# The tail of a decode layer: softmax sums ahead of the last PV, an output projection moved under a multiply, a shorter LN mean

## The chip, the cores and the metric

One core of one Trainium2 chip runs the whole program. Times are device microseconds (us), the median of several executions. The span that a profile shows, from the first to the last instruction, is about 1.8 us shorter than the time of the same execution. A verdict compares executions of fast state alone, with a 95% interval.

## The reference, cut to what matters

Two sequences decode one token through one layer. Attention reads the last 2048 positions of K and V for 32 heads of 192; then come the output projection, the residual, a second LayerNorm and a GELU feed-forward part.

```python
W = min(4096, max(256, Sk // 4))                     # Sk = 8192, so W = 2048
q = (x @ wq).reshape(B, Sq, Hq, Dh).transpose(0, 2, 1, 3)   # B=2, Sq=1, Hq=32, Dh=192
scores = jnp.einsum("bhqd,bhkd->bhqk", q, k[:, :, Sk - W:]) * (Dh ** -0.5)
o = jnp.einsum("bhqk,bhkd->bhqd", softmax(scores), v[:, :, Sk - W:])
h = x + o.reshape(B, Sq, Hq * Dh) @ wo               # D = 640; x is layer-normed ahead of wq
h2 = h + (gelu(ln(h) @ w_gate) * (ln(h) @ w_up)) @ w_down    # F = 1536
```

All tensors are bf16. Nearly all the bytes are K, V and weights, 122 MB, and each is used once.

## The kernel before

PE is TensorE (matmuls), DVE is VectorE and ACT is ScalarE; a load has landed when all of it is in SBUF. PV is the product of the exp of the scores with V. The o rows are its results summed into rows; the orow multiply divides them by the sums of exp and spreads them over the heads; the o columns are the same values turned, so that they can be multiplied with `wo`. The h columns and h rows are the residual sum h in the two layouts that the LayerNorm and the output need.

The kernel records its operations with the tiles they read (R), write (W) and the PSUM banks they touch (X); waits between engines follow from that. All loads but the small x go through one ring in SBUF and one DMA queue; the last of them, in a fixed order, are the end of K and V (16 steps, of which four make a group J of eight heads), then `wo` of heads 16 to 23, `wo` of heads 24 to 31, gate, up, and down in four quarters. After the last V nothing streams but the rest of these weights. The tail from there on is what the change rewrites.

```python
        def pv(g):
            ...                                  # 32 matmuls into ops_
            if g % 4 == 3:
                act(lambda e: e.activation(out=osb[:, :], in_=ops_[:, 0:384], func=ACT.Copy), W=["osb"], X=["o"])

        def o_rows(J):
            def fn(e):
                for tp in range(2):
                    e.matmul(m1[:, 0:DH], lhsT=selw[:, tp, :], rhs=osb[:, DH * tp:DH * (tp + 1)], ...)
                return e.matmul(m2[:, 272:276], lhsT=zsel[:, :], rhs=zr[:, J % 2, :], start=True, stop=True)
            pe(fn, ...)                          # o rows, then the sums of exp
            ...                                  # DVE: z4, rinv, wm
            dve(tt(orow[:, :, :], m1[:, 0:DH]..., wm[:, :]..., ALU.mult), R=["wm"], W=["orow"], X=["m1"])
        ...
        o_rows(3)
        o_columns(3)                             # 12 matmuls, then a small copy to ot
        oproj(2)                                 # wo of heads 16 to 23, into bank m1
        oproj(3)                                 # wo of heads 24 to 31, then hrow = m1 + hrow
        h_columns()
        layernorm(hT, "hT", hnT[:, :, :].unsqueeze(2), "hnT")
        ...
        ffn_in(sps, "s", "wg")                   # gate
        pe(h_rows, ...)                          # h into the bank of the output
        gT = ffn_columns(sps, "s", 0)            # an ACT and a DVE copy, then 3 transposes
        ...
        ffn_in(ops_, "o", "wu")                  # up, then down in four groups
```

(Cuts are marked by dots.)

Of the kernel before, what the change touches and what calls it, by code (L numbers as in the profile page):

```python
# [6 lines left out]
F32 = mybir.dt.float32  # L7
I32 = mybir.dt.int32
ALU = mybir.AluOpType
# [3 lines left out]
B = 2  # L13
# [137 lines left out]
def bass_sequential_preLN__sliding_block_cached__geglu_ffn__decode_kernel(  # L151
# [12 lines left out]
    with ExitStack() as ctx:  # L164

        def sb(name, shape, dt):
            return ctx.enter_context(nc.sbuf_tensor(name, shape, dt))
# [39 lines left out]
        lt = sb("lt", [128, 2, B], F32)  # L207
        xnT = sb("xnT", [128, NC5, 136], BF16)
        hnT = sb("hnT", [128, NC5, B], BF16)
        hT = sb("hT", [128, NC5, B], F32)  # L210
        qrow = sb("qrow", [128, 2, 2, DH], BF16)
        rq = sb("rq", [128, NG, 6, 16], BF16)
        mx = sb("mx", [128, 1], F32)
# [143 lines left out]

        dve(lambda e: e.memset(xnT[:, :, :].rearrange("p a b -> p (a b)").bitcast(I32), 0), W=["xnT"])

        def layernorm(src, src_tok, dst, dst_tok):  # L360
            dve(lambda e: e.tensor_reduce(out=ls[:, 0, :], in_=src[:, :, :].rearrange("p c b -> p b c"), axis=AX.X,
                                          op=ALU.add), R=[src_tok], W=["ls0"])
            pe(lambda e: e.matmul(m2[:, 16:18], lhsT=onesd[:, :], rhs=ls[:, 0, :], start=True, stop=True),
               R=["onesd", "ls0"], X=["m2"])
            dve(tt(dT[:, 0, :, :], src[:, :, :], m2[:, 16:18].unsqueeze(1).to_broadcast([128, NC5, B]), ALU.subtract),
                R=[src_tok], W=["dT0"], X=["m2"])
            dve(tt(dT[:, 1, :, :], dT[:, 0, :, :], dT[:, 0, :, :], ALU.mult), R=["dT0"], W=["dT1"])
            dve(lambda e: e.tensor_reduce(out=ls[:, 1, :], in_=dT[:, 1, :, :].rearrange("p c b -> p b c"), axis=AX.X,
                                          op=ALU.add), R=["dT1"], W=["ls1"])
            pe(lambda e: e.matmul(m2[:, 20:22], lhsT=onesd[:, :], rhs=ls[:, 1, :], start=True, stop=True),  # L370
               R=["onesd", "ls1"], X=["m2"])
            act(lambda e: e.activation(out=lt[:, 0, :], in_=m2[:, 20:22], func=ACT.Ln, bias=eps_t[:, :], scale=1.0),  # L372
                R=["eps"], W=["lt0"], X=["m2"])
            act(lambda e: e.activation(out=lt[:, 1, :], in_=lt[:, 0, :], func=ACT.Exp, scale=-0.5), R=["lt0"], W=["lt1"])
            n = dst.shape[2]
            dve(tt(dst, dT[:, 0, :, :].unsqueeze(2).to_broadcast([128, NC5, n, B]),
                   lt[:, 1, :].unsqueeze(1).unsqueeze(1).to_broadcast([128, NC5, n, B]), ALU.mult), R=["dT0", "lt1"], W=[dst_tok])
# [6 lines left out]

        pe(_x_T, R=["xrow", "identb"], X=["m2"])
        dve(lambda e: e.tensor_copy(xT[:, :, :].rearrange("p c b -> p (c b)"), m2[:, 0:10]), W=["xT"], X=["m2"])
        layernorm(xT, "xT", xnT[:, :, :].rearrange("p c (j x) -> p c j x", j=4)[:, :, :, 0:B], "xnT")


        dve(tt(pti[:, :], pi[:, :].to_broadcast([128, 11]), bits[:, :], ALU.bitwise_and),  # L390
# [44 lines left out]
        def consts_late():  # L435
            dve(ts(oh4[:, :], cf[:, 0, 0:4], pg[:, 8:9], ALU.is_equal), R=["cf0", "cq"], W=["oh4"])
            dve(ts(cf[:, 1, :], cf[:, 1, :], 2.0, ALU.mult), R=["cfm", "mska"], W=["cf1"])
            dve(ts(cf[:, 4, :], cf[:, 4, :], 0.25, ALU.mult), R=["cfm"], W=["cf4"])
            dve(tt(cf[:, 1, :], cf[:, 1, :], cf[:, 4, :], ALU.add), R=["cf1", "cf4"], W=["cf1"])
            dve(ts(cf[:, 3, :], cf[:, 3, :], 1000.0, ALU.mult), R=["cfm", "pm"], W=["cf3"])  # L440
            dve(tt(cf[:, 1, :], cf[:, 1, :], cf[:, 3, :], ALU.add), R=["cf1", "cf3"], W=["cf1"])
            for tp in range(2):
                dve(ts(selw[:, tp, :], cf[:, 1, :], float(tp), ALU.add, rb(31), ALU.is_equal), R=["cf1", "pf"], W=[("selw", tp)])
            for h in range(2):
                dve(ts(hsel[:, h, :], cf[:, 0, 0:2], 32.0 * h, ALU.add, pg[:, 12:13], ALU.is_equal), R=["cf0", "c63"], W=[("hsel", h)])
            dve(ts(pg[:, 8:9], rb(32), 1.0 / 32.0, ALU.mult), R=["pf", "cqb", "oh4"], W=["cb"])
            dve(ts(selb[:, :], cf[:, 0, 0:2], pg[:, 8:9], ALU.is_equal, pg[:, 2:3], ALU.mult), R=["cf0", "cb", "v4"], W=["selb"])
            dve(ts(maskhd[:, :], cf[:, 0, 0:8], pg[:, 10:11], ALU.is_equal, pg[:, 2:3], ALU.mult),
                R=["cf0", "chd", "v4"], W=["maskhd"])
# [109 lines left out]
        def pv(g):  # L559
            vv, vtoks = where["v", g]  # L560

            def fn(e):
                for t in range(32):
                    r = t % 4
                    ins = e.matmul(ops_[32 * r:32 * (r + 1), 0:384], lhsT=ering[:, g % 4, t, :],  # L565
                                   rhs=vv[:, 384 * t:384 * (t + 1)], start=(g % 4 == 0 and t < 4),
                                   stop=(g % 4 == 3 and t >= 28),
                                   tile_position=(0, 32 * r), skip_group_check=True)
                return ins

            pe(fn, R=[("er", g % 4)] + vtoks, X=["o"])
            done(("v", g))
            if g % 4 == 3:
                act(lambda e: e.activation(out=osb[:, :], in_=ops_[:, 0:384], func=ACT.Copy), W=["osb"], X=["o"])

        def o_rows(J):
            def fn(e):
                for tp in range(2):
                    e.matmul(m1[:, 0:DH], lhsT=selw[:, tp, :], rhs=osb[:, DH * tp:DH * (tp + 1)], start=(tp == 0),  # L579
                             stop=(tp == 1), skip_group_check=True)  # L580
                return e.matmul(m2[:, 272:276], lhsT=zsel[:, :], rhs=zr[:, J % 2, :], start=True, stop=True)

            pe(fn, R=["osb", "zsel", ("selw", 0), ("selw", 1)] + [("zr", J % 2, k) for k in range(4)], X=["m1", "m2"])
            dve(lambda e: e.tensor_tensor_reduce(out=z4[:, :], in0=m2[:, 272:276], in1=oh4[:, :], scale=1.0, scalar=0.0,
                                                 op0=ALU.mult, op1=ALU.add, accum_out=zs[:, :]), R=["oh4"], W=["z4", "zs"], X=["m2"])
            dve(lambda e: e.reciprocal(rinv[:, :], zs[:, :]), R=["zs"], W=["rinv"])
            dve(ts(wm[:, :], maskhd[:, :], rinv[:, 0:1], ALU.mult), R=["maskhd", "rinv"], W=["wm"])
            dve(tt(orow[:, :, :], m1[:, 0:DH].unsqueeze(1).to_broadcast([128, 8, DH]),
                   wm[:, :].unsqueeze(2).to_broadcast([128, 8, DH]), ALU.mult), R=["wm"], W=["orow"], X=["m1"])

        def o_columns(J):
            def fn(e):
# [7 lines left out]
        def oproj(J):  # L600
# [16 lines left out]
            done(("wo", J))  # L617
            if J == 0:
                dve(lambda e: e.tensor_copy(hrow[0:98, :], m1[0:98, 192:512]), W=["hrow"], X=["m1"])
            if J % 2:  # L620
                dve(tt(hrow[0:98, :], m1[0:98, 192:512], hrow[0:98, :], ALU.add), R=["hrow"], W=["hrow"], X=["m1"])

        def h_columns():
            def fn(e):
                for c in range(NC5):
                    for h in range(2):
                        ins = e.matmul(m2[64 * h:64 * h + 64, 32 + 2 * c:34 + 2 * c], lhsT=hrow[0:98, c:320:NC5],
                                       rhs=hsel[0:98, h, :], start=True, stop=True, tile_position=(0, 64 * h))
                return ins

            pe(fn, R=["hrow", ("hsel", 0), ("hsel", 1)], X=["m2"])
            dve(lambda e: e.tensor_copy(hT[:, :, :].rearrange("p c b -> p (c b)"), m2[:, 32:42]), W=["hT"], X=["m2"])


        transposes(0, 0)
# [6 lines left out]
        for g in range(NG):  # L642
            nxt = g + 1 < NG
            J = g // 4 - 1 if g % 4 == 0 and g > 0 else None
            if nxt:
                transposes(g + 1, 0)
            e_columns(g)
            if J is not None:
                o_columns(J)
            if nxt:  # L650
# [8 lines left out]
            if nxt:  # L659
                softmax(g + 1)  # L660
        o_rows(3)
        o_columns(3)
        oproj(2)
        oproj(3)

        h_columns()
        layernorm(hT, "hT", hnT[:, :, :].unsqueeze(2), "hnT")

        def ffn_in(bank, xt, key):
            wv, wtoks = where[key]  # L670
# [8 lines left out]
            pe(fn, R=["hnT"] + wtoks, X=[xt])  # L679

        def ffn_columns(bank, xt, i):
            act(lambda e: e.activation(out=grow[0:98, 192:384], in_=bank[0:98, 192:384], func=ACT.Copy), W=[("grow", 1)], X=[xt])
            dve(lambda e: e.tensor_copy(grow[0:98, 0:192], bank[0:98, 0:192]), W=[("grow", 0)], X=[xt])

            def fn(e):
                for j in range(3):
                    ins = e.transpose(tps[i][:, 128 * j:128 * j + 98], grow[0:98, j:384:3], identf[0:98, 0:98])  # L687
                return ins

            pe(fn, R=[("grow", 0), ("grow", 1), "identf"], X=[("t", i)])  # L690
            return tps[i][:, 0:384].rearrange("p (j r y) -> p r j y", j=3, y=32)[:, :, :, 0:2]

        def h_rows(e):
# [6 lines left out]
            return t.rearrange("p (r j b) -> p r j b", r=4, j=3)  # L700

        ffn_in(sps, "s", "wg")
        pe(h_rows, R=["hrow", ("hsel", 0), ("hsel", 1)], X=["m1"])
        gT = ffn_columns(sps, "s", 0)
        dve(lambda e: e.tensor_copy(rjb(gsb[:, :]), gT), W=["gsb"], X=[("t", 0)])
        dve(tt(ga[:, 0, :], gsb[:, :], gsb[:, :], ALU.mult), R=["gsb"], W=["ga0"])
        dve(ts(ga[:, 1, :], ga[:, 0, :], 0.044715, ALU.mult, 1.0, ALU.add), R=["ga0"], W=["ga1"])
# [83 lines left out]
```

## Time and profile before

The time is 297.32 us (three executions, 297.21 to 297.4). One execution was profiled; it took 298.14, its span is 296.4. This is 0.8 above the median.

The page of the kernel before, first line and the rows of its 40 slices: granted clock of PE and DMA share in tenths, and GB/s.

```profile
span 296.4 us, 4893 instructions
...
PEclk9996559996979589989788699979795979795555
DMA  7999999999999999999999999999999999999980
GB/s 272 435 446 433 425 425 427 428 427 435 437 413 442 428 426 417 435 437 429 427 429 433 423 425 437 431 427 425 431 430 428 423 438 430 428 424 427 423 359 37
...
```

DMA is busy throughout, at about 427 GB/s, and stops near 290 us. The last four slices have the clock of PE at half (5).

The chain of waits of the kernel before, from 255 us on (start, duration, what).

```profile
...
235.05 32.67 DMA ring<-in_A_v_cache_dram
...
267.85 2.77 PE ops L565 x32
...
271.19 1.65 PE m L579 x4
...
273.77 1.77 DVE orow L324
...
275.59 0.86 PE m L594 x12
276.45 3.33 PE m L611 x48
...
280.35 1.32 PE m L627 x20
...
284.80 1.80 PE sps L675 x15
...
288.22 1.73 PE ops L675 x20
...
291.93 1.80 PE m L722 x48
...
```

Up to 267.7 us the chain is a load. From there on it goes from engine to engine: PV, o rows, the orow multiply, o columns, both `wo` parts in one row of 48 matmuls, h columns, gate, up, down. No load stands in this part of the chain. The landings, taken from the trace's transfer records, say how near they are:

| weights | landed | first use in this profile | to spare |
|---|---|---|---|
| wo of heads 16 to 23 | 272.30 | 276.38 | 4.1 |
| wo of heads 24 to 31 | 276.89 | 277.93 | 1.05 |
| gate | 281.51 | 284.80 | 3.3 |
| up | 286.11 | 288.15 | 2.0 |
| down, last quarter | 290.79 | after 291.93 | over 1.1 |

### The profile page before, as it was taken

Reading aid. Unit: us, or ns where it says so; the run is one execution under the profiler, and the core shown is the slowest. Engines: PE = TensorE matmul, PEld = TensorE weight load, DVE = VectorE, ACT = ScalarE, POOL = GpSimd, SP = SyncE. Lnnn points to the kernel's source line nnn. Section 1 sums busy time; section 2 is a strip of 40 time slices with the busy share of each in tenths; the row PEclk is TensorE's granted clock in tenths of the full one; section 3 lists DMA queues with packets and bytes.
Section 4 is the critical chain, followed back from the end, with each engine's and each line's share of the span. In section 5 each row is a group of like instructions: output and inputs, shape, how many; then the busy total and the mean of one; then the engine's idle time right before and its main releaser. Section 6 shows DMA issues by size and latency. Waiting matters only on the chain.

```text
span 296.4 us, 4893 instructions
## 1 busy us (share of the span) xinstructions
PE 199.5 (67%) x2141; PEld 155.9 (53%) x2141; DVE 127.9 (43%) x316; ACT 98.4 (33%) x125; POOL 2.7 (1%) x19
## 2 busy tenths in 40 slices
PE   2573668849595398749492787576777885856764
PEld 1451266719393386547481766274757683834432
DVE  5950456614355154435344355334463543441222
ACT  2150134714353053416171325334334353330010
POOL 3000000000000000000000000000000000000000
PEclk9996559996979589989788699979795979795555
DMA  7999999999999999999999999999999999999980
GB/s 272 435 446 433 425 425 427 428 427 435 437 413 442 428 426 417 435 437 429 427 429 433 423 425 437 431 427 425 431 430 428 423 438 430 428 424 427 423 359 37
DMA packets 6521, 122.61 MB, mean 414 GB/s; under 512 B 738, under 2 KB 740, under 8 KB 1252
## 3 DMA queue, kind: packets, MB, share of 16 engines
q1 hardware_dynamic: 6488, 122.29, 96.8%
q8 instruction: 17, 0.28, 0.4%
q14 instruction: 4, 0.03, 0.0%
q10 hardware_dynamic: 12, 0.00, 0.0%
HBM read 122.29 MB, written 0.00 MB: 413 GB/s over the span
## 4 chain that ended last, share of the span: by engine, by line
DMA 69%; PE 24%; DVE 4%; ACT 1%; issue 1%; SPq 1%; DVEq 0%; ACTq 0%
DMA ring<-in_A_k_cache_dram 37%; DMA ring<-in_A_v_cache_dram 22%; PE tps L467 14%; DMA ring<-in_A_wq_dram 9%; PE ops L565 3%; PE m L611 1%; DVE rq L324 1%; PE m L594 1%; SPq L269 1%; PE m L722 1%; PE sps L675 1%; DVE orow L324 1%; PE ops L675 1%; PE m L579 1%; PE tps L687 1%
## 5 line engine op out<-in xcount | busy, mean ns | idle before, releaser
L467 PE MATMUL tps<-identf,ring 128*128 128x128 f32 x768 | 117.4, 323 | 47.4 <-DMA ring<-in_A_k_cache_dram 46.8
L467 PEld LDWEIGHTS tps<-identf,ring 128*128 128x128 f32 x768 | 108.2, 169 | 50.5 <-DMA ring<-in_A_k_cache_dram 48.1
L476 ACT ACTIVATE ktr<-tps 128x1024 bf16<-128x1024 bf16 x80 | 79.5, 1023 | 85.1 <-PE tps L467 85.1
L479 DVE COPY ktr<-tps 128x1024 bf16<-128x1024 bf16 x112 | 74.1, 688 | 74.3 <-PE tps L467 73.3
L540 ACT ACTIVATE eexp<-sm,nm 128x512 bf16<-128x512 f32 x16 | 11.5, 721 | 65.2 <-DVE nm L538 65.2
L565 PE MATMUL ops<-ring,ering 128*32 128x384 bf16 x512 | 25.0, 339 | 6.1 <-DMA ring<-in_A_v_cache_dram 6.0
L529 DVE CUSTOM_DVE_ANT_1 sm<-sps,mska 128x512 f32<-128x512 f32 x16 | 11.1, 691 | 40.2 <-PE sps L523 40.2
L523 PE MATMUL sps<-ktr,rq 128*16 128x512 bf16 x384 | 25.8, 403 | 0.3 <-DVE rq L324 0.3
L565 PEld LDWEIGHTS ops<-ring,ering 128*32 128x32 bf16 x512 | 12.9, 99 | 15.0 <-DMA ring<-in_A_v_cache_dram 6.4
L523 PEld LDWEIGHTS sps<-ktr,rq 128*16 128x16 bf16 x384 | 9.5, 90 | 11.3 <-issue 2.0
L536 PEld LDWEIGHTS m<-mrhs,pm 128*128 128x128 bf16 x16 | 1.5, 96 | 24.2 <-DVE mrhs L320 23.2
L536 PE MATMUL m<-mrhs,pm 128*128 128x16 bf16 x16 | 2.9, 184 | 16.8 <-DVE mrhs L320 16.0
L489 PE MATMUL tps<-ring,xnT 128*32 128x384 bf16 x80 | 5.7, 444 | 7.6 <-DMA ring<-in_A_wq_dram 7.6
L324 DVE TENSOR_TENSOR rq<-ops,mask 128x96 bf16<-128x96 f32 x16 | 2.7, 246 | 14.6 <-PE ops L507 14.6
L324 DVE TENSOR_TENSOR ering<-m,mask 128x256 bf16<-128x256 f32 x16 | 6.7, 420 | 3.5 <-PE m L549 3.5
L489 PEld LDWEIGHTS tps<-ring,xnT 128*32 128x32 bf16 x80 | 2.4, 120 | 10.4 <-DMA ring<-in_A_wq_dram 8.3
L324 DVE TENSOR_TENSOR orow<-m,wm 128x1536 bf16<-128x1536 f32 x4 | 7.0, 1757 | 0.1
L594 PE MATMUL m<-selb,orow 128*128 128x2 bf16 x48 | 3.4, 199 | 4.1 <-DVE orow L324 2.5
L372 ACT ACTIVATE lt<-m,eps_t 128x2 f32<-128x2 f32 x2 | 0.5, 262 | 16.8 <-PE m L370 16.8
L549 PE MATMUL m<-sel,eexp 128*128 128x64 bf16 x64 | 5.1, 207 | 1.2 <-ACT eexp L540 1.2
L549 PEld LDWEIGHTS m<-sel,eexp 128*128 128x128 bf16 x64 | 4.8, 112 | 1.7 <-DVE nm L538 1.3
L594 PEld LDWEIGHTS m<-selb,orow 128*128 128x128 bf16 x48 | 3.1, 159 | 4.6 <-DVE orow L324 2.6
(107 smaller groups left out, 81.3 us busy)
## 6 DMA issues: line engine op xcount, KB each, us to landing
ring<-in_A_k_cache_dram SPq DMA_DIRECT2D x16, 3072.0 KB, 26.6
ring<-in_A_v_cache_dram SPq DMA_DIRECT2D x16, 3072.0 KB, 30.1
ring<-in_A_wo_dram SPq DMA_DIRECT2D x4, 1920.0 KB, 30.9
ring<-in_A_wq_dram SPq DMA_DIRECT2D x2, 3072.0 KB, 21.1
ring<-in_B_w_gate_dram SPq DMA_DIRECT2D x1, 1920.0 KB, 33.7
ring<-in_B_w_up_dram SPq DMA_DIRECT2D x1, 1920.0 KB, 25.6
ring<-in_B_w_down_dram SPq DMA_DIRECT2D x4, 480.0 KB, 27.5
ring<-in_A_wq_dram SPq DMA_DIRECT2D x1, 1536.0 KB, 27.9
```

What stands on the lines that cost most here:

```text
L324: return lambda e: e.tensor_tensor(out=out, in0=a, in1=b, op=op)
L467: ins = e.transpose(tps[bi][:, 128 * u:128 * (u + 1)], kv[:, off:off + 128], identf[:, :])
L476: act(lambda e, dst=dst, bv=bv: e.activation(out=dst, in_=bv, func=ACT.Copy), W=[("kt", slot, n)], X=[("t", bi)])
L479: dve(lambda e, dst=dst, bv=bv: e.tensor_copy(dst, bv), W=[("kt", slot, n)], X=[("t", bi)])
L489: ins = e.matmul(tps[0][32 * r:32 * (r + 1), 0:384], lhsT=xnT[:, c, 32 * J:32 * (J + 1)], rhs=wq[:, c - c0, 1536 * J + 384 * r:1536 * J + ...
L523: ins = e.matmul(sps[32 * ch:32 * ch + 16, :], lhsT=rq[:, g, k, :], rhs=ktr[:, g % 2, k // 2, 1024 * ch + k % 2:1024 * (ch + 1):2], start= ...
L529: dve(lambda e: e.tensor_tensor_reduce(out=sm[:, :].rearrange("p (u x) -> p u x", u=4), in0=sps[:, :].rearrange("p (u x) -> p u x", u=4), ...
L540: act(lambda e: e.activation(out=eexp[:, :], in_=sm[:, :], func=ACT.Exp, bias=nm[:, 0:1], scale=1.0, accum_out=zr[:, g // 4 % 2, g % 4:g % ...
L549: ins = e.matmul(o, lhsT=eexp[:, 128 * u:128 * (u + 1)], rhs=sel64[:, :], start=True, stop=True)
L565: ins = e.matmul(ops_[32 * r:32 * (r + 1), 0:384], lhsT=ering[:, g % 4, t, :], rhs=vv[:, 384 * t:384 * (t + 1)], start=(g % 4 == 0 and t < 4),
L594: ins = e.matmul(m2[:, 2 * kk:2 * kk + 2], lhsT=orow[:, :, kk:DH:12], rhs=selb[:, :], start=True, stop=True)
L675: ins = e.matmul(bank[32 * r:32 * r + 2, 0:384], lhsT=hnT[:, c, :], rhs=wv[:, c, 384 * r:384 * (r + 1)], start=(c == 0), stop=(c == NC5 - ...
```

## The change

It has three parts. **Front:** the sums of exp, their inverse and the head mask `wm` are made before the last PV; `osb` is copied by DVE in two halves, so that the first o-row matmul can start behind the first half; the last o rows go to the bank of the scores, which leaves bank m1 free, so that `wo` of heads 16 to 23 is multiplied while DVE spreads the o rows. **Mean:** the hrow addition also sums its rows; one matmul makes the LN mean from these sums, right behind the h columns, and the copy hT goes. **FFN:** one DVE copy in place of an ACT and a DVE copy, and the h rows stand behind the gate's transposes.

```diff
-                act(lambda e: e.activation(out=osb[:, :], in_=ops_[:, 0:384], func=ACT.Copy), W=["osb"], X=["o"])
+                for tp in range(2):
+                    dve(lambda e, tp=tp: e.tensor_copy(osb[:, DH * tp:DH * (tp + 1)], ops_[:, DH * tp:DH * (tp + 1)]), ...)
...
+        def z_rows(J):                           # matmul of the sums, z4, rinv, wm: taken out of o_rows
...
+            bank, tok = (m1, "m1") if J < 3 else (sps, "s")
...
+            if J == 3:
+                dve(lambda e: e.tensor_tensor_reduce(out=hrow[0:98, :], in0=m1[0:98, 192:512], in1=hrow[0:98, :], ...,
+                                                     op0=ALU.add, op1=ALU.add, accum_out=rs[0:98, :]), ...)
...
-            dve(lambda e: e.tensor_copy(hT..., m2[:, 32:42]), W=["hT"], X=["m2"])
...
             e_columns(g)
+            if g % 4 == 3:
+                z_rows(g // 4)
...
         o_rows(3)
+        oproj(2)
         o_columns(3)
-        oproj(2)
         oproj(3)
 
         h_columns()
-        layernorm(hT, "hT", hnT[:, :, :].unsqueeze(2), "hnT")
+        layernorm(m2[:, 32:42]..., [], ["m2"], hnT[:, :, :].unsqueeze(2), "hnT",
+                  lambda e: e.matmul(m2[:, 16:18], lhsT=rs[0:98, :].to_broadcast([98, 128]), rhs=bsel[0:98, :], ...))
...
-            act(lambda e: e.activation(out=grow[0:98, 192:384], in_=bank[0:98, 192:384], func=ACT.Copy), ...)
-            dve(lambda e: e.tensor_copy(grow[0:98, 0:192], bank[0:98, 0:192]), ...)
+            dve(lambda e: e.tensor_copy(grow[0:98, :], bank[0:98, 0:384]), W=["grow"], X=[xt])
...
         ffn_in(sps, "s", "wg")
+        gT = ffn_columns(sps, "s", 0)
         pe(h_rows, R=["hrow", ("hsel", 0), ("hsel", 1)], X=["m1"])
-        gT = ffn_columns(sps, "s", 0)
```

Why the two copies of an eviction stood in sequence before, and why the last o rows need another bank for `wo` to run meanwhile: the program makes an operation wait for the last one of any other engine on the same bank (X), reads included. The trace of before agrees: ACT's half of the gate's copy runs from 286.62 to 286.95, DVE's starts at 287.05.

## The prediction

> **What bounds the kernel.** The page shows DMA 90% busy or more in nearly every slice up to slice 38, at about 427 GB/s[...], so nothing can be won while K and V stream. The chain of waits runs through DMA to 267.7 us, when the last V lands. Then comes a serial tail of 28.7 us: PV, o rows, o columns, wo, LN, FFN. The change shortens this tail alone. But weights still stream under it. By the transfer records they land at: wo of heads 16–23 272.3, wo of 24–31 276.9, gate 281.5, up 286.1, down 287.3/288.5/289.6/290.8. These times don't depend on the change. Before, the uses begin at 276.4, about 278.1, 284.8, 288.2 and 291.9.

> **The sum** (timeline and chain; the clock granted in the tail is 0.5):
> 1. Sums of exp ahead of PV: the z matmul (0.23) and z, inverse, wm (about 0.9) leave the chain. The osb copy goes from one ACT copy (0.50) to two DVE copies of about 0.36 (as the 98x192 copy took), the second behind the first o-row matmul: about even. The orow multiply starts near 272.75 instead of 273.77: −1.0.
> 2. wo of 16–23 (1.67 of the 3.33) runs under the orow multiply (1.76), in another bank. So o columns end near 275.4 and wo of 24–31 could start near 275.7, 2.4 earlier than before. But its weights land at 276.9: it starts near 277.0 and ends near 278.7 instead of 279.75. Of about 2.1 us, steps 1 and 2 together keep 1.1.
> 3. The hrow add becomes an add with a row sum (a 512-wide one took 0.69 plus its accumulator read; for 320 I estimate 0.58 against 0.49): +0.1.
> 4. Mean: hT copy, reduce and their hand-overs go. The mean matmul follows on the h columns (as the z matmul did, about 0.25), then a small mean copy (0.17): −0.6. The gate matmuls start near 283.2, not 284.8.
> 5. FFN evictions: ACT 0.34 then DVE 0.37 in sequence (same bank) become one DVE copy of 384; from 192 (0.36) and 320 (0.49) columns I estimate 0.56: −0.25 for gate, −0.25 for up.
> 6. h rows now stand behind the gate's transposes, so 0.53 of them falls between those and the up matmuls, where before they filled the eviction wait: +0.5.

> Up starts near 286.9 (landed 286.1), down near 290.4; its last quarter is needed near 291.7 (landed 290.8). No further weight binds. Elsewhere (three earlier o rows, x's LN, one more constant) the work lies under DMA: 0.

> −1.1 +0.1 −0.6 −0.25 +0.5 −0.25 = −1.6; I say 1.5.

> **Predicted:** 295.8 us, range 295.1 to 296.7. Faster by over 2% (below 291.4) 0.01, within 2% 0.98, slower 0.01. Even with all compute of the tail free, the last down weights at 290.8 plus output leave at most some 2.5 us.

> **Right if:** the first o-row matmul starts near 271.1 and orow near 272.75; wo of 24–31 waits for DMA, with PE idle over 1 us after the o columns; gate starts at 283.2±0.3; the h rows lie between transposes and up; landings are unchanged within 0.3; final copy ends near 292.5.

> **Wrong if:** the added DVE work in the K stages delays a load's issue (landings shift); wo of 24–31 doesn't wait; the row-sum add or the mean matmul costs much more than estimated; or up or down starts waiting for its weights.

(The cut took out a ceiling for DMA that no trace of this case shows. That nothing can be won while K and V stream then rests on the busy share alone and is the author's estimate. No term of the sum is cut: it came to −1.6, and 1.5 was said.)

## The result, and the profile after

| | median us | executions | lowest to highest |
|---|---|---|---|
| before | 297.36 | 6 | 297.21 to 297.73 |
| changed | 297.02 | 6 | 296.43 to 297.19 |

The ratio is 0.9983, with an interval of 0.997 to 0.9996. (A ratio is the mean time of one kernel's fast runs over that of the other's in the same rounds, so not quite the ratio of the medians; "slower" executions below are still fast runs, 0.3% apart from the rest.) The change is a gain, of 0.34 us by the medians and 0.5 by the ratio (interval 0.1 to 0.9), where 1.5 was predicted; 297.02 lies above the predicted range, which ends at 296.7.

The page of the changed kernel, first line and the rows of its slices.

```profile
span 295.2 us, 4895 instructions
...
PEclk9995959997979689977998697979599979599555
DMA  7999999999999999999999999999999999999991
...
```

The chain of waits of the changed kernel, from 230 us on (start, duration, what).

```profile
...
247.30 29.64 DMA ring<-in_A_wo_dram
...
277.07 1.80 PE m L622 x23
...
279.45 1.30 PE m L641 x20
280.75 0.53 PE m L683 x2
...
283.56 1.80 PE sps L691 x20
...
285.38 0.57 DVE grow L698
...
286.75 0.65 PE m L710 x8
287.40 1.62 PE ops L691 x20
...
290.76 1.80 PE m L737 x45
...
```

In these two profiles the gain is 296.36 − 295.25 = 1.1 us, and most events behind the o rows are close to those predicted: gate starts at 283.56 (predicted 283.2±0.3), `wo` of heads 24 to 31 now stands in the chain as a load (landed 276.94, matmuls from 277.07), the h rows stand between transposes and up. No landing moved by more than 0.06 us against before. So the profiles tell of 1.1 us and the timed medians of 0.34. The question is where the rest went.

The profile after has a second oddity. Here is its tail's front in the timeline (start, duration, engine, line, operation, what it makes from what; in brackets how long the engine was idle before it, and for whom).

```profile
...
267.97 1.48 PE L572 MATMUL ops<-ring,ering 128*32 128x384 bf16 x32
...
269.50 0.62 DVE L582 COPY osb<-ops 128x192 f32<-128x192 f32 x2 [0.79 <-PE ops L572]
...
269.91 0.92 PE L597 MATMUL sps<-osb,selw 128*128 128x192 f32 x4 [0.46 <-DVE osb L582]
270.94 1.76 DVE L326 TENSOR_TENSOR orow<-sps,wm 128x1536 bf16<-128x1536 f32 x1 [0.82 <-PE sps L597]
...
272.38 1.57 PE L622 MATMUL m<-ring,ot 128*2 128x320 bf16 x24 [1.55 <-DMA ring<-in_A_wo_dram]
...
277.07 1.77 PE L622 MATMUL m<-ring,ot 128*2 128x320 bf16 x24 [2.31 <-DMA ring<-in_A_wo_dram]
...
```

PV took 1.48 us and the o rows 0.92, where the profile of before has 2.75 and 1.65. The same 32 and 4 matmuls do the same work in both kernels. The clock was full here (1.00 from 258.98 to 272.63), half there (0.50 from 266.94 to the end), and so the first o-row matmul came at 269.91 where 271.1 was predicted. And despite that advantage of 2 us, PE then waited 1.55 us for the first `wo` part and 2.31 us for the second.

### The profile page after: what moved, and what is told of

It is laid out like the page before. It is cut to its first block, busy times and chain, and to the rows that moved or that the text cites. A ratio compares the mean times of both kernels' runs of the same rounds, so it can differ in the third digit from the quotient of the medians.

```text
span 295.2 us, 4895 instructions
## 1 busy us (share of the span) xinstructions
PE 194.2 (66%) x2141; PEld 152.0 (51%) x2141; DVE 130.2 (44%) x326; ACT 95.6 (32%) x119; POOL 2.7 (1%) x19
## 4 chain that ended last, share of the span: by engine, by line
DMA 69%; PE 24%; DVE 4%; issue 1%; SPq 1%; ACT 0%; DVEq 0%; ACTq 0%
DMA ring<-in_A_k_cache_dram 50%; PE tps L474 17%; DMA ring<-in_A_wo_dram 10%; DMA ring<-in_A_wq_dram 9%; PE m L622 1%; PE ops L572 1%; DVE rq L326 1%; PE m L737 1%; PE sps L691 1%; PE m L605 1%; SPq L271 1%; PE ops L691 1%; PE tps L702 1%; DVE ktr L486 0%; PE m L641 0%
## 5 line engine op out<-in xcount | busy, mean ns | idle before, releaser
L474 PE MATMUL tps<-identf,ring 128*128 128x128 f32 x768 | 115.3, 319 | 50.0 <-DMA ring<-in_A_k_cache_dram 49.3
L572 PE MATMUL ops<-ring,ering 128*32 128x384 bf16 x512 | 23.7, 327 | 3.8 <-DMA ring<-in_A_v_cache_dram 3.7
L530 PE MATMUL sps<-ktr,rq 128*16 128x512 bf16 x384 | 24.8, 390 | 0.3 <-DVE rq L326 0.3
L496 PE MATMUL tps<-ring,xnT 128*32 128x384 bf16 x80 | 5.1, 406 | 6.8 <-DMA ring<-in_A_wq_dram 6.8
L622 PE MATMUL m<-ring,ot 128*2 128x320 bf16 x96 | 5.3, 371 | 3.9 <-DMA ring<-in_A_wo_dram 3.9
L326 DVE TENSOR_TENSOR orow<-m,wm 128x1536 bf16<-128x1536 f32 x3 | 5.3, 1750 | 0.0
L622 PEld LDWEIGHTS m<-ring,ot 128*2 128x2 bf16 x96 | 2.3, 95 | 5.7 <-issue 2.5
```

Source lines behind the costliest of these rows:

```text
L326: return lambda e: e.tensor_tensor(out=out, in0=a, in1=b, op=op)
L474: ins = e.transpose(tps[bi][:, 128 * u:128 * (u + 1)], kv[:, off:off + 128], identf[:, :])
L496: ins = e.matmul(tps[0][32 * r:32 * (r + 1), 0:384], lhsT=xnT[:, c, 32 * J:32 * (J + 1)], rhs=wq[:, c - c0, 1536 * J + 384 * r:1536 * J + ...
L530: ins = e.matmul(sps[32 * ch:32 * ch + 16, :], lhsT=rq[:, g, k, :], rhs=ktr[:, g % 2, k // 2, 1024 * ch + k % 2:1024 * (ch + 1):2], start= ...
L572: ins = e.matmul(ops_[32 * r:32 * (r + 1), 0:384], lhsT=ering[:, g % 4, t, :], rhs=vv[:, 384 * t:384 * (t + 1)], start=(g % 4 == 0 and t < 4),
L622: ins = e.matmul(m1[32 * r:32 * r + 2, 192:512], lhsT=ot[:, J % 2, kk, :], rhs=wo[:, kk, 320 * h:320 * (h + 1)], start=(kk == 1 or J > 0 a ...
```

## The experiments

The experiments ran in three groups, each on one chip and with runs of before that its kernels share: before again and the parts alone; the two splits of the `wo` load, the early h rows and both together; the doubled multiply, the kept-busy PE and the two last looks. The changed kernel itself was timed in none of them, so a difference of medians from its 297.02 is one between groups; the ratios to before are the sounder comparison.

### Before again, and each part of the change alone

Theory A: the profile of before that I predicted from was a slow draw, its half clock hid a wait that most executions have. Rival B: it was typical, and the gain is lost outside of the span.

**Before, unchanged.**

> The kernel before, unchanged, for more of its executions and a second profile. Theory A (the profile of before that I predicted from was a slow draw: PV ran at half clock there, 2.75 us, and so hid a wait for wo of heads 24 to 31 that most executions have): spans mostly near 295.5 us, not 296.4; in the new profile PV takes about 1.5 us and the second half of the wo matmuls starts at about 277.07, just after those weights land at 276.9. Rival B (the profile of before is typical, and the changed kernel loses the rest of its gain outside the span, before the first or after the last instruction): spans of before near 296.4, PV 2.75 us again, no wait for wo.

Measured: median 297.69 us (five executions) against 297.16 for nine others of the same kernel in the same rounds; ratio 1.0011, interval 0.9997 to 1.0025. The spans of the five: 296.3, 295.5, 295.4, 296.0, 295.9; of the nine: 296.1, 295.3, 295.5, 295.2, 295.4, 295.0, 295.4, 295.9, 295.4. Most are near 295.5, as theory A says, and B falls, since span and time differ by 1.8 us in all. But the execution that happened to be profiled was again one of the long ones (296.3), PV took 2.63 us in it, and no wait for `wo` is seen. So this half of A was not shown yet. Note too that the five and the nine are the same kernel, and that their medians differ by 0.53 us: which kind of execution is drawn more often moves a median by more than the change did.

**Front alone.** The edit is the first, second, third and sixth piece of the diff above, and the move of `oproj(2)` in the seventh.

> Only the first part of the change: sums and inverse ahead of PV, osb by two DVE copies, last o rows in the scores bank, wo of 16 to 23 under the orow multiply; LN and FFN as before. The prediction gave this part -1.1 us. Theory A: 0.0 (within 0.15 us), as both kernels then start wo of 24 to 31 at its landing. Rival B: -1.1 in the span.

Measured: 297.12 us, ratio 0.9996 (0.9983 to 1.0008). The part that should have given 1.1 us gives nothing that five rounds can see. Its profile (span 295.3), PE's rows of the timeline:

```profile
...
267.68 2.75 PE L565 MATMUL ops<-ring,ering 128*32 128x384 bf16 x32 [0.58 <-DMA ring<-in_A_v_cache_dram]
270.90 1.65 PE L590 MATMUL sps<-osb,selw 128*128 128x192 f32 x4 [0.47 <-DVE osb L575]
...
276.94 1.77 PE L615 MATMUL m<-ring,ot 128*2 128x320 bf16 x24 [1.61 <-DMA ring<-in_A_wo_dram]
...
```

PV and the o rows are both at half clock, as in the first profile of before, and yet `wo` of heads 24 to 31 waits 1.61 us for its load, which landed at 276.81.

**Mean alone.** The edit is `bsel`, the row-sum addition, the new `layernorm` and the loss of hT.

> Only the LN part: row sums out of the hrow add, mean by one matmul behind the h columns, no hT copy. The prediction gave -0.5 (-0.6 and +0.1). The stretch from the end of wo to the first gate matmul took 5.02 us in the trace of before and 4.69 in that of the changed kernel, so theory A expects -0.33 us, all of it kept, as it lies behind the wait for wo; under B the same.

Measured: 296.63 us, ratio 0.9985 (0.9973 to 0.9998). From the end of `wo` to the first gate matmul its trace has 278.99 to 283.70, 4.71 us, against 279.75 to 284.80, 5.05 us, in the trace of before.

**FFN alone.** The edit is the last two pieces of the diff.

> Only the FFN part: one DVE copy per eviction, h rows behind the gate's transposes. Predicted 0.0 (-0.25, +0.5, -0.25). From the first gate matmul to the first down matmul the two traces have 7.13 us before and 7.20 after: expected +0.07 us, under A and B alike.

Measured: 297.28 us, ratio 1.0004 (0.9991 to 1.0016). No gain, as expected. Gate to down took 7.20 us in its trace, the same as in the changed kernel.

The product of the three ratios is 0.9985, that of the whole change 0.9983. As far as intervals of about 0.4 us to either side can tell, the parts add up, and the gain in the median is that of the shorter LN mean.

### Is the load of `wo` what the front runs into?

**The load of `wo` of heads 24 to 31 in four, on the kernel before.** Each quarter has its own six matmuls and its own wait.

```diff
-        load_wo(3)
+        for i in range(4):
+            load(("wo", 3, i), 2 * 3 * D, A_wo[4608:6144, :].rearrange("(p kk) n -> p kk n", kk=12)[:, 3 * i:3 * (i + 1), :], ...)
```

> The kernel before, with the load of wo of heads 24 to 31 split into four (and its matmuls into four groups that each wait for their own quarter). It needs the weights no later and no earlier; only the wait for the whole load goes. Theory A': most executions of before wait for this load, some (PV at half clock, as in both profiles of before so far) don't. So the median falls by about 1 us (in the waiting ones the last quarter starts at 277.0 and wo ends near 277.5 instead of 278.85), and the slowest executions, spans of 296 and over, stay or fall least. Rival C: before never waits for this load, the front part's gain went elsewhere: 0 within 0.15 us.

Measured: 297.26 us, ratio 0.9981 (0.9964 to 0.9999). Not what A' expected: the median hardly moved. The spans are 295.5, 295.5, 294.6, 295.5, 296.1, 294.8. Two of the six, 294.6 and 294.8, lie below every span recorded of the unchanged kernel (295.0 and more) and pull the ratio below 1, though the median stays; the others did not gain. So A', "most executions of before wait for this load", falls; that the two would have waited is likely, but they were not profiled. The profiled one (295.5) shows a third kind: PV at half clock (2.74), o rows at full clock (0.97), then all 48 `wo` matmuls in a row from 275.48 to 278.86, without a wait. It is the end that matters: 278.86, where the changed kernel, which does wait, ends at 278.84.

**The same split on the changed kernel.**

> The changed kernel with the load of wo of heads 24 to 31 in four. Under A' every execution of the changed kernel waits for that load (wo starts 277.07, ends 278.87): now the last quarter alone starts at 277.07 and wo ends near 277.5, 1.3 us earlier. Further on the up weights (286.15) cost about 0.2 and the last down weights (290.81) leave at most 1.15: -1.0 to -1.15 us. Rival C: 0.

Measured: 296.18 us, ratio 0.9952 (0.994 to 0.9964), that is 0.84 below the median of the changed kernel. The last two quarters in PE's rows of its timeline:

```profile
...
276.06 0.43 PE L627 MATMUL m<-ring,ot 128*2 128x320 bf16 x6 [0.45 <-DMA ring<-in_A_wo_dram]
277.29 0.58 PE L627 MATMUL m<-ring,ot 128*2 128x320 bf16 x6 [0.80 <-DMA ring<-in_A_wo_dram]
...
```

So the changed kernel does wait for this load, and a finer load takes much of the wait away: `wo` ends at 277.87 instead of 278.84. It gives less than the 1.3 us expected there since the four loads took longer than the one: the last quarter landed 9.5 us after the last V, the whole load 9.2 us after it in the trace of the changed kernel, and the last down weights landed at 291.08 instead of 290.81.

**Making the front of the changed kernel worse on purpose.** The last orow multiply is done twice.

```diff
+            if J == 3:
+                dve(tt(orow[:, :, :], bank[:, 0:DH]..., wm[:, :]..., ALU.mult), R=["wm"], W=["orow"], X=[tok])
             dve(tt(orow[:, :, :], bank[:, 0:DH]..., wm[:, :]..., ALU.mult), R=["wm"], W=["orow"], X=[tok])
```

> The changed kernel with the last orow multiply done twice (1.76 us more on the chain between PV and the o columns). If the front of the changed kernel ends in a wait for wo of 24 to 31 with 1.9 us or more to spare, this costs 0.0 us (within 0.1): o columns end near 275.5 to 276.6, still ahead of 276.9. If the front is what sets the time, +1.7 us.

Measured: 296.96 us, ratio 0.998 (0.9967 to 0.9993), the same as the changed kernel without it. The timeline of its profile:

```profile
...
272.06 3.55 DVE L326 TENSOR_TENSOR orow<-sps,wm 128x1536 bf16<-128x1536 f32 x2 [1.47 <-PE sps L597]
...
275.68 0.88 PE L608 MATMUL m<-selb,orow 128*128 128x2 bf16 x12 [2.37 <-DVE orow L326]
...
277.04 1.77 PE L625 MATMUL m<-ring,ot 128*2 128x320 bf16 x24 [0.48 <-DMA ring<-in_A_wo_dram]
...
```

The two multiplies take 3.55 us, the o columns come nearly two microseconds later than in the changed kernel, and the second `wo` part starts at 277.04 as ever, still after a wait for its load. An added 1.76 us on the front costs nothing; so a saving on it cannot be worth anything either, beyond the point at which this wait begins.

### What makes the executions of before differ?

**Before, with PE kept busy while it waits for the last V.**

```diff
+        def idle_work(n):                        # n matmuls of 512 columns into a free bank, read by nobody
...
+            if g == NG - 1:
+                idle_work(7)
             pv(g)
```

(Four more each stand behind the last scores and behind the last row maximum.)

> The kernel before, with 15 matmuls of 512 columns that nobody reads, placed on PE while it waits for the last V (7 of them just ahead of PV), so that the granted clock should stay full through PV. Five traces with the front of before show PV at half clock; their spans are 296.3 (o rows at half clock too) or 295.5 (o rows at full clock), and 25 timed executions fall into the same two groups. Theory D (the clock's windows run free of the program; where they fall decides whether the front of before costs 0.85 us more, and my profile was of the dearer kind): PV takes 1.5 us, o columns end near 274.5, now the second half of wo waits for its weights (276.9) and ends at about 278.85: all spans 295.3 to 295.5, no group at 296, median 0.0 to -0.1 against the median of before, and about -0.3 in the mean. Rival E (the spread of before has another cause, such as the transfers): both groups stay.

Measured: 297.34 us, ratio 0.9994 (0.9981 to 1.0008); spans 295.4, 295.7, 295.6, 295.4, 295.5. The nine runs of before beside it had three of 296.0 and 296.1; this kernel had none, which five executions could also show by chance (about one time in eight if a third is slow). The timeline of its profile, PE's rows:

```profile
...
268.53 1.48 PE L565 MATMUL ops<-ring,ering 128*32 128x384 bf16 x32
270.61 0.92 PE L579 MATMUL m<-osb,selw 128*128 128x192 f32 x4 [0.60 <-ACT osb L574]
...
274.16 0.88 PE L594 MATMUL m<-selb,orow 128*128 128x2 bf16 x12 [2.52 <-DVE orow L324]
274.97 0.99 PE L611 MATMUL m<-ring,ot 128*2 128x320 bf16 x24
276.99 1.77 PE L611 MATMUL m<-ring,ot 128*2 128x320 bf16 x24 [1.03 <-DMA ring<-in_A_wo_dram]
...
```

PV and o rows run at full clock, 1.48 and 0.92 us, although the added work made PV start 0.7 us late. The first `wo` part takes 0.99 us. And then the second waits 1.03 us for its load and starts at 276.99. The front of before itself, when the clock is kind, ends in the very wait that the changed kernel has. Its median is no better than that of before.

**Two more looks at the unchanged kernel.**

> One more look at the unchanged kernel before. Theory D: if the span is near 295.4, PV or the o rows run at full clock and wo ends near 278.85; if near 296.2, both at half clock and wo ends near 279.7. Rival E: the span and the clock in the stretch from 267.7 to 273 don't go together.

> A further look, with the same two outcomes as the one before it: span near 295.4 with a full clock in PV or the o rows, or near 296.2 with half clock in both.

Measured: spans 295.7 and 295.3 (single runs, but both lie among the fast spans of before). PE's rows in the timeline of the first:

```profile
...
267.99 2.75 PE L565 MATMUL ops<-ring,ering 128*32 128x384 bf16 x32 [1.81 <-DMA ring<-in_A_v_cache_dram]
271.33 0.92 PE L579 MATMUL m<-osb,selw 128*128 128x192 f32 x4 [0.59 <-ACT osb L574]
...
274.89 0.86 PE L594 MATMUL m<-selb,orow 128*128 128x2 bf16 x12 [2.52 <-DVE orow L324]
275.68 3.37 PE L611 MATMUL m<-ring,ot 128*2 128x320 bf16 x48
...
```

And the clock in the window in which PV runs and in the next, by the view of windows; first in the first profile of before (window, its length, busy time of each engine, then PEclk, DMA share and GB/s).

```profile
...
core 0: us, PE busy (x) PEld busy (x) DVE busy (x) ACT busy (x) POOL busy (x), PEclk, DMA share, GB/s
266.94:270.35 3.41, 2.50 (x32) 1.28 (x32) 0.00 (x0) 0.00 (x0) 0.00 (x0) 0.50 1.02 428
270.35:273.77 3.42, 2.13 (x10) 1.78 (x6) 0.57 (x4) 0.49 (x1) 0.00 (x0) 0.50 1.00 422
...
```

The same two windows in the first look, with the same columns.

```profile
...
267.83:271.24 3.41, 2.75 (x32) 1.28 (x32) 0.00 (x0) 0.45 (x1) 0.00 (x0) 0.50 1.01 428
271.24:274.66 3.42, 1.03 (x6) 0.95 (x6) 2.15 (x5) 0.04 (x1) 0.00 (x0) 1.00 1.01 422
...
```

The look at 295.7 has PV at half clock and the o rows at full. The second look, 295.3, has the reverse: PV 1.84 us, o rows 1.65. The six traces that have the program of before up to `wo`, without added work and without the split, and that of the changed kernel:

| trace | PV us | o rows us | wo 24–31 landed | its matmuls start | behind the landing | span |
|---|---|---|---|---|---|---|
| before | 2.75 | 1.65 | 276.89 | 277.93 | 1.05 | 296.4 |
| before again | 2.63 | 1.65 | 276.90 | 277.81 | 0.91 | 296.3 |
| mean alone | 2.75 | 0.92 | 276.89 | 277.17 | 0.28 | (295.3) |
| FFN alone | 2.75 | 0.92 | 276.76 | 277.00 | 0.24 | (295.5) |
| first look | 2.75 | 0.92 | 277.04 | 277.23 | 0.19 | 295.7 |
| second look | 1.84 | 1.65 | 277.17 | 277.31 | 0.13 | 295.3 |
| changed kernel | 1.48 | 0.92 | 276.94 | 277.07 | 0.13 | 295.2 |

(Spans in brackets are of kernels with other changes behind `wo`.) The changed kernel, whose trace shows it waiting, starts 0.13 us behind the landing, so this much is the hand-over itself. So the front could gain 0.9 us in the first row and 0.15 or less in the four ordinary ones. The loads do not land later in the two slow traces (276.89 and 276.90) than in the four others (276.76 to 277.17), which speaks against rival E. Of 36 executions of the unchanged kernel whose spans were recorded in the experiments, 12 are 295.9 or longer and 24 at most 295.7. The clock that the record has for each execution (the mean over its span) goes with them: 0.809 to 0.824 in the 12, 0.822 to 0.846 in the 24. In the six executions of the changed kernel it ranges from 0.816 to 0.852, and both ends have a span of 295.2: between these two the clock makes no difference. (A mean over the span is a pointer only; it does not say where the clock was low.) Of 16 executions with the new front (the changed kernel, the front alone, the doubled multiply), none is above 295.5. So far as these runs show, that is all the front does: it removes the slow third, and leaves the median where it was.

### What the h rows cost, and the best that came of it

**The changed kernel with the h rows ahead of the gate.**

```diff
+        pe(h_rows, R=["hrow", ("hsel", 0), ("hsel", 1)], X=["m1"])
         ffn_in(sps, "s", "wg")
         gT = ffn_columns(sps, "s", 0)
-        pe(h_rows, R=["hrow", ("hsel", 0), ("hsel", 1)], X=["m1"])
```

> The changed kernel with the h rows ahead of the gate matmuls, where PE waits 0.85 us for the normalised h. If their 0.53 to 0.65 us between the gate's transposes and the up matmuls is what ate the gain of the single copies: -0.55 us, the down matmuls start near 290.2 instead of 290.76 (last weights 290.8). If the h rows were hidden, 0.

Measured: 296.43 us, ratio 0.9957 (0.9945 to 0.9969), 0.6 below the median of the changed kernel. Gate to down takes 6.71 us in its trace instead of 7.20, so 0.5 is the place of the h rows; the other 0.1 is within what separates groups of runs. PE waited for the normalised h at that place anyway (0.85 us ahead of the gate in the trace of the changed kernel, 0.21 behind the h rows in this one).

**Both.**

> The changed kernel with both: wo in four loads and the h rows early. The down matmuls would be ready near 289.2 but their last quarter lands at 290.81 and then takes about 0.45 us: -1.15 to -1.2 us, hardly more than the split alone, as the end is now set by the last weights. If it gives 1.7 us, the landing of the last weights doesn't bind as I think.

Measured: 296.12 us, ratio 0.9949 (0.9937 to 0.9961): the best, 1.3 us below the median of before in its rounds (297.42), and its five times lie within 0.13 us. Against the median of the changed kernel (297.02) that is 0.9, less than the 1.15 expected; over the split alone it gives as little as expected, though for another reason than written. Its timeline:

```profile
...
286.30 1.77 PE L696 MATMUL ops<-ring,hnT 128*2 128x384 bf16 x20 [0.61 <-DMA ring<-in_B_w_up_dram]
...
289.85 1.77 PE L742 MATMUL m<-ring,uT 128*2 128x160 bf16 x48 [0.34 <-DVE uT L326]
...
```

The up matmuls wait 0.61 us for their weights, which landed at 286.26. I had named the last down weights (290.96); their matmuls came at the end of a row that began at 289.85, and show no wait. The last quarter of `wo` is waited for as well (0.48 us, at 277.11). In this version loads set the pace of the tail at two places.

## Why the prediction was wrong

- **What bounds the kernel** was right. DMA up to 267.7, a serial tail, weights landing under it at times that the change doesn't move: landings stayed within 0.06 us.
- **Steps 1 and 2 together (−1.1) is the term that failed.** The mechanism was right: the matmuls of `wo` of heads 24 to 31 wait for their load, and from profile to profile their end moved by 0.91 us, from 279.75 to 278.84. What was wrong is the time from which the saving was counted: the prediction let these matmuls begin at about 278.1 before the change, and in the ordinary traces of that front they begin at 277.00 to 277.31. The profile of before was one execution of the slower kind, with PV and o rows both at half clock. In the four ordinary traces one of them runs at full clock, and the front of before reaches this load 0.13 to 0.28 us behind its landing; two thirds of the executions have spans like theirs. There the term is 0.1, not 1.1; the front alone measured a ratio of 0.9996. The warning stood: the profiled execution was 298.14 where the median was 297.32. Had I taken that 0.8 off the one place where the luck of the clock could have put it, the term would have been 0.3.
- **Step 3 (+0.1)** was 0.01: from the end of `wo` to the h columns 0.60 us before, 0.61 after.
- **Step 4 (−0.6)** was −0.35: from the first h-column matmul to the end of the subtraction 2.57 us before, 2.22 after. The mean matmul adds 0.53 us behind the h columns in the chain, twice my 0.25. Steps 3 and 4 together: −0.34 in the trace, ratio 0.9985 alone.
- **Steps 5 and 6 (−0.25, +0.5, −0.25)** were right: 0.86 to 0.63 and 0.87 to 0.64 from matmul to transpose, and +0.5 for the h rows; sum +0.07 by the traces, ratio 1.0004 alone.
- **The sum of what was left**, −0.1, −0.34 and +0.07, is −0.37 us; the medians differ by 0.34. That they agree so closely is luck, as the interval is 0.4 us to either side. The ratio gives somewhat more (0.17% of 297, 0.5 us), which fits with the slow third being gone too.
- **What remains open:** the spread of 294.6 to 295.4 in the spans of the changed kernel was not followed up, and why one window's work brings the full clock and another's doesn't is not known (see the end).

## What to carry to other kernels

A profile is one execution: compare its time with the median before costing anything from it, and where they differ, take a second and third look before naming a saving. In a tail in which loads still land, write the landing beside each use; time saved ahead of a load is worth only what separates the use from the landing, in the ordinary execution and not in the slowest. A doubled cost that changes nothing shows in one run that a stage has slack, and once a load binds, splitting it (0.84 us here) or shortening the chain behind it (0.6) gains where speeding up the work before it does not.

## What else the traces show

- The busy share of PE in a window doesn't tell by itself which clock follows. Counted in windows of 3.41 us, from the first clock record on, in the traces of before and of the changed kernel: from half clock, windows with PE busy for 0.89 or more were followed by full clock and those with 0.73 or less by half clock again; between them both happened (0.79 was followed by full clock in the changed kernel, from 26.87; 0.82 by half clock in before, from 277.18). From full clock, the windows with 0.48 or more stayed full and those with 0.30 or less fell to half; between them 0.43 stayed full (changed kernel, from 142.92), and 0.42 (before, from 219.16 and 236.22) and 0.41 (changed kernel, from 269.22) fell.
- What costs here is a fall to half clock near the end. The two traces of before with PV and o rows both at half clock have spans of 296.4 and 296.3, the two with one of them at or partly at full clock 295.7 and 295.3. At 0.8 of 296 us (0.3%) it is small, but it is more than the change measured was worth (0.17%).
- With one core at work this kernel moved about 427 GB/s for some 280 us.
- Four loads of 0.49 MB in place of one of 1.97 MB, in the middle of a full queue, landed about 0.2 us later. In traces where both PV and the last `wo` matmuls wait for their load, the starts of the two are 9.49 us apart with four loads (the split on the changed kernel), 9.26 and 9.33 with one (the front alone, the early h rows).
